# Dense layer's input rows: transposed as 16-bit parts by DMA in place of TensorE, from the third pair of tiles on

## The chip, the core and the metric

The kernel runs on one core of a Trainium2 chip: TensorE (PE) for products, VectorE (DVE), ScalarE (ACT) and GpSimd (POOL) for element-wise work, SyncE (SP) as the queue that issues nearly all DMAs. The metric is the device time of one execution in microseconds, the median over runs.

## The reference

Three layers follow one another. Shapes: q, k, v are 4 x 8 x 768 x 64 (batch, heads, positions, head size); 3072 tokens of 512 values each leave attention.

```python
scores = (q @ k.T) / 8 - slope[h] * dist      # keys: 8 global ones and the 96 before the query
a = exp(scores - max); a = a / sum(a)
x = (a @ v), as 3072 rows x 512
h = max(x @ w1, x @ w2, x @ w3)               # dense layer, 768 wide
x2 = h @ w_out                                # 3072 x 512
e = argmax(x2 @ w_gate)                       # one of 8 experts per token
out = gate * sigmoid(x2 @ w_output_gate)[e] * (relu(x2 @ e_w1[e]) @ e_w2[e])   # 1024 wide
```

## The kernel before

Tokens are handled in 24 tiles of 128 rows. All wide products are made of three 16-bit products: each operand is kept as a high part and a low part (`low_of` computes the low part as scaled value minus high part, with a running sum for a check at the end).

The first stage interleaves attention and the dense layer. Attention goes tile by tile (u = 0 to 23): loads of q, k, v (L823, L821), transposes of q and k on PE (L903), scores (L955), minima and exponentials (L979, L986), a split of the probabilities into two 16-bit parts (L1000), a DMA transpose of these (`a_trans`, L1006), products with v (L1036), and a scaled result `xo` (L1042) that is stored to a DRAM buffer `xd` (L1048).

The dense layer goes in 12 passes over pairs of tiles. `m_load(p, t)` fetches tile t of pair p: for the first two pairs (`NEARLY = 2`) the tile is still in SBUF, later ones are reloaded from `xd` (L1077). PE transposes its four 128x128 blocks in fp32 into a PSUM bank (L1089), ACT writes the scaled high part from there (L1092), DVE the low part (L1094, shown at L200). Both go to one of two `xT` buffers, and a pass needs both tiles of its pair. `m_1` makes the products with w1, w2, w3 (L1125); `m_max` takes maxima; `m_2` makes the product with w_out (L1182), writes its result as two 16-bit parts `x2r`, and transposes these through `rows_T` (L1218), a DMA transpose issued by SP (L1223; for the last pair PE does it). `m_route` then chooses experts and scatters the rows.

The order of all of this is made by a planner, the class `Plan`, when the program is built: tasks are generators that yield operations with an engine, an estimated cost and the buffers that they read and write; the planner picks the operation that can start first by its estimates (rank breaks ties), and the instructions are emitted in that order. On the chip each engine, SP's queue too, runs its own list in that fixed order and waits on semaphores. Buffers come from stocks: `take` waits for one, `give` returns it.

After the lists of tokens per expert are made, a loop over experts (L1881) runs to the end.

Of the kernel before, what the change touches and what calls it, by code (L numbers as in the profile page):

```python
# [9 lines left out]
F32 = mybir.dt.float32  # L10
F32R = mybir.dt.float32r
F16 = mybir.dt.float16
# [3 lines left out]
ALU = mybir.AluOpType  # L16
# [4 lines left out]
P = 128  # L21
# [11 lines left out]
NEARLY = 2  # L33
# [17 lines left out]
XS = 2.0**13  # L51
# [16 lines left out]
class Plan:  # L68
# [24 lines left out]
    def state(self, *fact):  # L93
        self.facts.add(fact)

    def give(self, tag, buf):
        buf.free = buf.last
        self.idle.setdefault(tag, []).append(buf)

    @staticmethod  # L100
    def need(*facts):
        return ("need", facts)

    @staticmethod
    def take(tag):
        return ("take", tag)

    @staticmethod
    def op(eng, cost, r=(), w=(), tail=None, port=True):
        return ("op", eng, cost, r, w, tail, port)  # L110
# [87 lines left out]
def low_of(nc, out, x, scale, high, total):  # L198

    nc.vector.scalar_tensor_tensor(out=out, in0=x, scalar=scale, in1=high, op0=ALU.mult, op1=ALU.subtract, accum_out=total)  # L200


def dense_attention(tc, q, k, v, vd, ngl, nlo, ident):

    nc = tc.nc
    B, H, S, HD = q.shape
    QT = S // P
    HS = S // 2
    with tc.tile_pool(name="da", bufs=1) as da, tc.tile_pool(name="db", bufs=1) as db, tc.tile_pool(
        name="dps", bufs=2, space=PSUM  # L210
# [4 lines left out]
        dist = da.tile([P, QT, S], F32, name="ddist")  # L215
        mask = da.tile([P, QT, S], F32, name="dmask")
# [1 line left out]
        nc.vector.tensor_scalar(out=mask, in0=dist, scalar1=0.0, scalar2=None, op0=ALU.is_ge)  # L218
        nc.vector.scalar_tensor_tensor(out=mask, in0=dist, scalar=nlo, in1=mask, op0=ALU.is_lt, op1=ALU.mult)
        nc.vector.tensor_mul(out=dist, in0=dist, in1=mask)  # L220
        for i in range(0, QT, 2):
            far = db.tile([P, 2, S], F32, tag="far", name="dfar")
            nc.vector.tensor_scalar(out=far, in0=mask[:, i : i + 2], scalar1=0.0, scalar2=nlo, op0=ALU.is_equal, op1=ALU.mult)
            nc.vector.tensor_add(out=dist[:, i : i + 2], in0=dist[:, i : i + 2], in1=far)
        nc.vector.tensor_max(out=mask, in0=mask, in1=glo.unsqueeze(1).to_broadcast([P, QT, S]))
        nc.vector.tensor_scalar(out=mask, in0=mask, scalar1=-MASK, scalar2=MASK, op0=ALU.mult, op1=ALU.add)
        slopes = da.tile([P, H], F32, name="slopes")
# [2 lines left out]
        with tc.For_i(0, B, 1) as b, tc.For_i(0, H, 1) as h:  # L230
# [9 lines left out]
            for src, dst, sc in ((qn, qT, -1.0 / HD**0.5), (kn, kT, 1.0)):  # L240
                for c in range(QT):
                    pt = dps.tile([P, 512], F32, tag="dpt", name="dpt")
                    nc.tensor.transpose(pt[:HD, :P], src[:, c, :], ident)
                    nc.scalar.mul(out=dst[:, c * P : (c + 1) * P], in_=pt[:HD, :P], mul=sc)
            for i in range(QT):
                t = db.tile([P, S], F32, tag="dt", name="dt")
                for half in range(2):
# [4 lines left out]
                        out=t[:, ks], in0=dist[:, i, ks], scalar=slope, in1=sc[:, :HS], op0=ALU.mult, op1=ALU.add  # L252
# [4 lines left out]
                    out=t, in0=t, in1=mask[:, i], scale=1.0, scalar=3.0e38, op0=ALU.add, op1=ALU.min, accum_out=mn[:, 0:1]  # L257
# [5 lines left out]
                for c in range(QT):  # L263
                    pt = dps.tile([P, 512], F32, tag="dpt", name="dpa")
# [3 lines left out]
                for c in range(QT):  # L268
# [4 lines left out]
                    out=vd[bass.ds(b, 1), bass.ds(h, 1), i * P : (i + 1) * P, :].rearrange("o u p d -> p (o u d)"), in_=o  # L273
# [105 lines left out]
def local_attention_moe_kernel(  # L379
# [17 lines left out]
    nc = tc.nc  # L397
    B, H, S, HD = q.shape
    NT, D = out.shape
    FF = w1.shape[1]  # L400
    E, _, FE = e_w1.shape
    KD = D // P
    KF = FF // P
    KE = FE // P
    QT = S // P
# [14 lines left out]
    ident = cp.tile([P, P], F32, name="ident")  # L420
# [17 lines left out]
    chk = cp.tile([P, -(-(A_OK + 8) // LINE) * LINE], F32, name="chk")  # L438
    late = ExitStack()
    big = late.enter_context(tc.tile_pool(name="big", bufs=1))  # L440
    mo = late.enter_context(tc.tile_pool(name="mo", bufs=1))
# [19 lines left out]
    with tc.manual_schedule(engines={mybir.EngineType.SP, mybir.EngineType.Activation}):  # L461
# [3 lines left out]
        for j, src in enumerate((q, k, v)):  # L465
            t = first_t[j // 2][:, j % 2 * D : (j % 2 + 1) * D]
# [31 lines left out]
    def window(nf, neg, gl):  # L498

        nc.vector.tensor_scalar(out=neg, in0=nf, scalar1=0.0, scalar2=4294967296.0, op0=ALU.is_lt, op1=ALU.mult)  # L500
        nc.vector.tensor_add(out=neg, in0=neg, in1=nf)
        nc.vector.scalar_tensor_tensor(out=gl, in0=nf[:, 1::2], scalar=4294967296.0, in1=neg[:, ::2], op0=ALU.mult, op1=ALU.add)
        return gl[:, 0:1], gl[:, 1:2]
# [7 lines left out]
    with tc.If(dense > 0):  # L511
        nf = cp.tile([P, 4], F32, name="nf")
        nc.vector.tensor_copy(out=nf, in_=nw)
        ngl, nlo = window(nf, neg, gl)
        dense_attention(tc, q, k, v, vd, ngl, nlo, ident)
# [5 lines left out]
    ngl, nlo = seen_gl[:, 0:1], seen_gl[:, 2:3]  # L521
# [3 lines left out]
    op, need, take, give, state = plan.op, plan.need, plan.take, plan.give, plan.state  # L525
    PE, DVE, ACT, POOL, DMA = "PE", "DVE", "ACT", "POOL", "DMA"

    def stock(tag, tiles, bank=False):
        for t in tiles:
            plan.idle.setdefault(tag, []).append(Buf(t, bank))  # L530
# [7 lines left out]
    def act(n):  # L538
        return 0.17 + n * 0.00085

    def dve(n):
        return 0.155 + n * 0.00104
# [4 lines left out]
    def psum(cost, r=(), w=()):  # L547

        return op(DVE, cost, r, w, port=False)

    def dma(nbytes, r=(), w=(), held=False, rate=DMA_RATE):
        return op(DMA, 0.5, r, w, tail=(0.06 + nbytes / rate, held))
# [29 lines left out]
    x2_all = mo.tile([P, 3 * XB], F32, name="x2r")  # L582
    x2_t = [x2_all[:, n * XB : n * XB + XW] for n in range(3)]
    stock("x", x_t)
    stock("x2s", [mo.tile([P, 2 * KD, 2 * P], F16, name="x2s")])
    stock("hm", hm_t)

# [476 lines left out]
    def m_load(p, t):  # L1064
        c = passes[p][0]
        n = CHUNKS[c][t]
        seq = X_SEQ[p] + t
        yield need(("o", n), *([("x", seq - 1)] if seq else []), *([("xT", p - 1)] if p else []))
        if p < NEARLY:
            xb = M["x", n]  # L1070
            state("x", seq)
        else:
            xb = yield take("x")
            state("x", seq)
            xb.free = max(xb.free, X_AT[n])
            yield dma(P * D * 4, w=[xb])
            nc.sync.dma_start(out=xb.t, in_=xd[n * P : (n + 1) * P, :])  # L1077
        if t == 0:
            M["xT", p] = yield take("xT")
            state("xT", p)  # L1080
        yield need(("xT", p))
        yield op(DVE, 0.2, [xb], [])
        nc.vector.tensor_reduce(out=chk[:, A_L + n : A_L + n + 1], in_=xb.t[:, :NLOW], axis=AX.X, op=ALU.max)
        xT = M["xT", p]
        bank = yield take("bank")
        pt = bank.t.rearrange("p (a b) -> p a b", b=P)
        for d in range(KD):
            yield op(PE, 0.109, [xb], [bank])
            nc.tensor.transpose(pt[:, d, :], xb.t[:, d * P : (d + 1) * P], ident)  # L1089
        h, l = [x[:, :, t * P : (t + 1) * P] for x in xT.t]  # L1090
        yield op(ACT, act(D), [bank], [xT])
        nc.scalar.mul(out=h, in_=pt, mul=XS)  # L1092
        yield psum(dve(D) + 0.07, [bank, xT], [xT])
        low_of(nc, l, pt, XS, h, chk[:, n : n + 1])  # L1094
        give("bank", bank)
        give("x", xb)
        state("xT", p, t)

    def m_banks():
# [118 lines left out]
    def rows_T(rows, src, dst, t, dstb, pe_, get=None):  # L1218

        at = dst[:, :, t * P : (t + 1) * P]  # L1220
        if not pe_:
            yield dma(P * 2 * D * 2, [src], [dstb], rate=DMA_RATE_ROWS)
            nc.sync.dma_start_transpose(out=at, in_=rows)  # L1223
            return
        bank = yield get()
        pt = bank.t.bitcast(F16).rearrange("p (a b) -> p a b", b=P)
        for d in range(2 * KD):
            yield op(PE, 0.06, [src], [bank])
            nc.tensor.transpose(pt[:, d, :], rows[:, d * P : (d + 1) * P], ident16)
        yield op(ACT, act(D), [bank], [dstb])  # L1230
        nc.scalar.copy(out=at[:, :KD], in_=pt[:, :KD])
        yield psum(dve(D), [bank], [dstb])
        nc.vector.tensor_copy(out=at[:, KD:], in_=pt[:, KD:])
        give("bank", bank)
# [586 lines left out]
    for p, (c, js) in enumerate(passes):  # L1821
        for t in range(len(CHUNKS[c])):
            plan.add(m_load(p, t), (1, p, -1, t), HOLD_M)
        plan.add(m_1(p), (4, p, 0), HOLD_F)
        if 2 in js:
            for t in range(len(CHUNKS[c])):
                plan.add(m_2(c, t), (4, c, 1 + t), HOLD_F)
# [12 lines left out]
    with tc.manual_schedule(engines={ET.PE, ET.Activation, ET.DVE, ET.Pool, ET.SP}):  # L1840

        reli, mask, tmp = [t[:, n * NW : (n + 1) * NW] for t, n in ((hm_t[0], 0), (hm_t[0], 1), (hm_t[1], 0))]
        key, rel, rel0, far, mask0, slopes = [hm_t[0][:, 2 * NW + n * NG : 2 * NW + (n + 1) * NG] for n in range(6)]
# [4 lines left out]
        for t, fill in ((rel, MASK), (rel0, 0.0)):  # L1848
            nc.gpsimd.affine_select(
                out=t, in_=rel0, pattern=[[-1, NG]], compare_op=ALU.is_ge, fill=fill, base=0, channel_multiplier=1  # L1850
# [3 lines left out]
        for j in range(2):  # L1854
# [4 lines left out]
            out=reli[:, NG:], in_=reli[:, NG:], pattern=band, compare_op=ALU.is_ge, fill=MASK, base=NPREV, channel_multiplier=1  # L1859
# [77 lines left out]
```

## Time and profile before

| what | value |
|---|---|
| median of 3 runs | 910.21 us (909.91 to 914.42) |
| profiled execution | 908.63 us, its span 907.1 us |
| PE busy | 829.1 us, 91% of the span |
| DVE busy | 641.0 us, 71% |
| ACT busy | 473.7 us, 52% |
| POOL busy | 197.8 us, 22% |
| DMA queue of SP | 65.1% of 16 engines' span |

The span runs from the first to the last instruction; the time of an execution contains a little more. Busy shares are means over stages: attention with dense products until about 450 us, dense products until about 570 us, experts from about 600 us on. PE's products are pipelined, so an instruction's duration is longer than the distance to the next one.

### The profile page before, as it was taken

The numbers are of one execution on the slowest core, as the hardware profiler recorded it, in microseconds if no ns is written. First come the engines' busy times: TensorE is split into PE (matmuls) and PEld (weight loads), VectorE is DVE, ScalarE is ACT, GpSimd is POOL, SyncE is SP. The second block draws the span as 40 slices with busy tenths as digits, with TensorE's granted clock in tenths as the row PEclk, the third lists the DMA queues.
The fourth block names the chain that finished last, engine by engine and source line by source line (L and its number), as shares of the span: only waits on it lengthen the run. The fifth ranks groups of instructions, "written<-read, shape, count | busy, mean of one in ns | idle before, by whom it ended". The sixth has DMA issues, their size and how long they took to land. (4 is left out here: it accounts for less than half of the span.)

```text
span 907.1 us, 23690 instructions
## 1 busy us (share of the span) xinstructions
PE 829.1 (91%) x8469; PEld 638.4 (70%) x8469; DVE 641.0 (71%) x1911; ACT 473.7 (52%) x994; POOL 197.8 (22%) x245
## 2 busy tenths in 40 slices
PE   3566799999999999999999999979999999989993
PEld 2456677787878786878778778747777766667671
DVE  5998968888788877877567523447677776657774
ACT  4776756667567666765344211205555555545551
POOL 3443332232324132211011011011111111111111
PEclk9968899999999999999999999989999999999997
DMA  7996459878797888874585131067888888888841
GB/s 206 267 252 198 106 89 205 177 189 182 159 197 188 172 209 170 185 165 99 130 322 143 24 60 36 13 233 214 245 256 255 255 247 243 260 247 246 246 133 38
DMA packets 271702, 164.58 MB, mean 181 GB/s; under 512 B 233824, under 2 KB 233824, under 8 KB 271620
## 3 DMA queue, kind: packets, MB, share of 16 engines
q1 hardware_dynamic: 267458, 150.91, 65.1%
q0 software_dynamic: 4160, 12.62, 3.8%
q8 instruction: 46, 0.75, 0.3%
q14 instruction: 36, 0.29, 0.1%
q10 hardware_dynamic: 2, 0.00, 0.0%
HBM read 118.56 MB, written 23.11 MB: 156 GB/s over the span
## 5 line engine op out<-in xcount | busy, mean ns | idle before, releaser
L1125 PE MATMUL bank<-xT,w 128*128 128x256 f16 x2592 | 306.4, 275 | 3.8 <-DVE xT L200 2.1
L1125 PEld LDWEIGHTS <-w 128*128 128x128 f16 x2592 | 250.4, 99 | 45.6 <-issue 9.8
L1689 PE MATMUL bank<-xT,we 128*128 128x128 f16 x2496 | 145.8, 222 | 13.2 <-DMA xT<-x2r 7.4
L1689 PEld LDWEIGHTS <-we 128*128 128x128 f16 x2496 | 143.8, 99 | 17.0 <-DMA xT<-x2r 8.3
L986 ACT ACTIVATE sp<-sp,mn 128x232 f32<-128x232 f32 (+1 forms) x192 | 89.8, 468 | 56.0 <-DVE mn L979 53.2
L1643 PEld LDWEIGHTS <-he 128*128 128x128 f16 x672 | 65.2, 98 | 75.7
L1632 ACT ACTIVATE hm<-bank 128x512 f32<-128x512 f32 x56 | 33.2, 593 | 137.3 <-PE bank L1689 121.3
L1182 PE MATMUL bank<-w,hh 128*128 128x512 f16 x432 | 101.0, 379 | 0.0
L1147 DVE SCALAR_TENSOR_TENSOR hm<-bank,hm 128x512 f32<-128x512 f32 x72 | 49.7, 690 | 57.8 <-PE bank L1125 55.0
L1643 PE MATMUL bank<-we,he 128*128 128x512 f16 x360 | 80.2, 379 | 0.0
L1182 PEld LDWEIGHTS <-hh 128*128 128x128 f16 x432 | 41.1, 98 | 40.7 <-issue 0.2
L1643 PE MATMUL bank<-wp,he 128*128 128x512 f16 x312 | 69.5, 379 | 0.0
L856 POOL TENSOR_SCALAR qkn<-qkn,vs 128x512 f32<-128x512 f32 x23 | 38.6, 1678 | 140.6 <-DVE vs L851 92.7
L200 DVE SCALAR_TENSOR_TENSOR wp<-ws,wp 128x1024 f16<-128x1024 f32 x56 | 65.2, 1220 | 0.0
L1319 POOL DMA_INDIRECT xs<-x2r,di x24 | 26.2, 1091 | 171.5 <-DVE x2r L1315 91.9
L979 DVE CUSTOM_DVE_ANT_0 sp<-bank,bias 128x232 f32<-128x232 f32 x160 | 60.5, 389 | 3.3 <-PE bank L955 3.2
L200 DVE SCALAR_TENSOR_TENSOR we<-ws,we 128x1024 f16<-128x1024 f32 x49 | 59.7, 1223 | 0.5
L955 PE MATMUL bank<-k,qh 64*128 64x232 f32 (+1 forms) x384 | 43.5, 317 | 18.0 <-ACT k L929 14.9
L195 POOL TENSOR_TENSOR seen<-x,dco 128x1 f32<-128x1 f32 x14 | 13.2, 940 | 208.6 <-DVE x L1648 208.6
L1574 ACT ACTIVATE wp<-ws 128x1024 f16<-128x1024 f32 x54 | 55.1, 1050 | 5.2 <-PE bank L1643 3.5
L1636 DVE CAST he<-hm 128x512 f16<-128x512 f32 x29 | 12.4, 427 | 62.7 <-ACT hm L1632 62.6
L195 DVE TENSOR_TENSOR nat<-sp,nat 128x928 f16<-128x928 f32 (+1 forms) x47 | 53.2, 1131 | 0.8
(260 smaller groups left out, 1232.7 us busy)
## 6 DMA issues: line engine op xcount, KB each, us to landing
ws<-in_moe_w_dram SPq DMA_DIRECT2D x112, 512.0 KB
raw<-in_moe_w_dram SPq DMA_DIRECT2D x12, 768.0 KB
bias<-in_moe_w_dram SPq DMA_DIRECT2D x16, 512.0 KB
x2r<-xs SPq DMA_DIRECT2D x30, 257.0 KB
qkn<-in_q_dram SPq DMA_DIRECT2D x23, 256.0 KB
qkn<-in_k_dram SPq DMA_DIRECT2D x23, 256.0 KB
qkn<-vd SPq DMA_DIRECT2D x23, 256.0 KB
qkn<-in_v_dram SPq DMA_DIRECT2D x23, 256.0 KB
```

What stands on the lines that cost most here:

```text
L195: eng.tensor_tensor(out=out, in0=in0, in1=in1, op=ALU.subtract)
L200: nc.vector.scalar_tensor_tensor(out=out, in0=x, scalar=scale, in1=high, op0=ALU.mult, op1=ALU.subtract, accum_out=total)
L856: nc.gpsimd.tensor_scalar(out=vf, in0=vf, scalar1=scale, scalar2=None, op0=ALU.mult)
L955: nc.tensor.matmul(sc[j][:, hp, :nw_], lhsT=x, rhs=y, start=(n < 2), stop=(n >= len(terms) - 2))
L979: nc.vector.tensor_tensor_reduce(out=o[:, g:], in0=x[:, g:], in1=bias[:, pr, n0 + g :], scale=scale, scalar=low, op0=ALU.add, op1=ALU.min, ...
L986: nc.scalar.activation(out=o, in_=o, func=AF.Exp, scale=-1.0, bias=mn[:, h : h + 1], accum_out=sm[:, h : h + 1])
L1125: nc.tensor.matmul(pj[:, f2, :], lhsT=w_at(j, part, d)[:, fs], rhs=X[:, d, :], start=(d + n == 0), stop=(d == KD - 1 and n == 2))
L1147: nc.vector.scalar_tensor_tensor(out=hv, in0=pj, scalar=1.0 / WS, in1=hv, op0=ALU.mult, op1=ALU.max)
L1182: nc.tensor.matmul(bank.t, lhsT=X[:, f, t * P : (t + 1) * P], rhs=w_at(3, part, f), start=(f + n == 0), stop=(f == KF - 1 and n == 2))
L1574: nc.scalar.mul(out=h, in_=s.t, mul=XS)
L1643: nc.tensor.matmul(py, lhsT=at(A_), rhs=w, start=(f + m == 0), stop=(last and m == 2))
L1689: nc.tensor.matmul(pg[:, f, :], lhsT=W[d][B_][:, fs], rhs=xT[A_][:, d, :], start=(d + m == 0), stop=(d == KD - 1 and m == 2))
```

## The change

For pairs from the third on, the tile is no longer transposed by PE. ACT writes the scaled high part of the untransposed tile to the left half of a new SBUF buffer `rows` (128 x 1024, 16 bit; one buffer), DVE the low part to the right half, the input buffer is given back, and `rows_T` issues one DMA transpose of all eight 128x128 blocks to the tile's place in `xT`. The buffer `rows` is given back to the planner after that transpose. Room for `rows` is made in a part that does not run with these inputs (`dense_attention`, used when the window is larger than the fast path's): its buffer `far` is halved.

```diff
-        for i in range(0, QT, 2):
-            far = db.tile([P, 2, S], F32, tag="far", name="dfar")
...
+        for i in range(QT):
+            far = db.tile([P, S], F32, tag="far", name="dfar")
...
     stock("x", x_t)
+    stock("rows", [mo.tile([P, 2 * D], F16, name="rows")])
...
         xT = M["xT", p]
-        bank = yield take("bank")
-        pt = bank.t.rearrange("p (a b) -> p a b", b=P)
-        for d in range(KD):
-            yield op(PE, 0.109, [xb], [bank])
-            nc.tensor.transpose(pt[:, d, :], xb.t[:, d * P : (d + 1) * P], ident)
...
+        if p < NEARLY:
...
+        else:
+            rows = yield take("rows")
+            yield op(ACT, act(D), [xb], [rows])
+            nc.scalar.mul(out=rows.t[:, :D], in_=xb.t, mul=XS)
+            yield op(DVE, dve(D) + 0.07, [xb, rows], [rows])
+            low_of(nc, rows.t[:, D:], xb.t, XS, rows.t[:, :D], chk[:, n : n + 1])
+            give("x", xb)
+            yield from rows_T(rows.t, rows, xT.full, t, xT, False)
+            give("rows", rows)
         state("xT", p, t)
```

The branch `p < NEARLY` holds the former lines unchanged.

## Rows read from the trace of the kernel before

**Rows 1.** The page: the span, and each engine's busy time.

```profile
span 907.1 us, 23690 instructions
PE 829.1 (91%) x8469; PEld 638.4 (70%) x8469; DVE 641.0 (71%) x1911; ACT 473.7 (52%) x994; POOL 197.8 (22%) x245
```

**Rows 2.** Busy time by stretches; last PE's granted clock, DMA share, GB/s.

```profile
150.00:450.00 300.00, 295.38 (x3145) 234.54 (x3146) 232.92 (x788) 186.85 (x496) 75.82 (x93) 1.00 0.78 173
450.00:607.00 157.00, 151.08 (x1213) 114.66 (x1211) 83.36 (x281) 40.84 (x70) 15.38 (x31) 0.99 0.36 108
```

**Rows 3.** Timeline of PE: start, length, operation, count, idle before and its releaser.

```profile
606.91 12.71 PE L1689 MATMUL bank<-xT,we 128*128 128x128 f16 x192 [5.77 <-SPq L1881]
```

**Rows 4.** Timeline of PE at the last pair's transposes.

```profile
500.76 0.60 PE L1089 MATMUL bank<-ident,x 128*128 128x128 f32 x4
501.20 0.60 PE L1089 MATMUL bank<-ident,wf 128*128 128x128 f32 x4
```

**Rows 5.** Instructions of line 1089, 169 to 605 us (ns: min/median/max).

```profile
L1089 PE MATMUL bank<-ident,x x44: 272/273/307, 188.2 to 501.1; 128*128 128x128 f32 x44
L1089 PE MATMUL bank<-ident,wf x28: 272/273/331, 169.2 to 501.5; 128*128 128x128 f32 x28
```

**Rows 6.** Timeline of PE at the start of the third pass.

```profile
163.87 1.15 PE L1125 MATMUL bank<-xT,w 128*128 128x256 f16 x9
...
169.15 0.66 PE L1089 MATMUL bank<-ident,wf 128*128 128x128 f32 x4 [1.21 <-DMA wf<-xd]
```

**Rows 7.** Groups by line: count, busy us, mean ns, idle before.

```profile
L1092 ACT ACTIVATE xT<-bank 128x512 f16<-128x512 f32 x24 | 14.0, 593 | 13.6 <-PE bank L1089 12.9 <-PE bank L842 0.7
L858 ACT CAST va<-qkn 128x512 f16<-128x512 f32 x23 | 14.1, 613 | 6.0 <-POOL qkn L856 5.9
L200 DVE SCALAR_TENSOR_TENSOR xT<-bank,xT 128x512 f16<-128x512 f32 x24 | 16.4, 687 | 3.7 <-ACT xT L1092 3.6
L200 DVE SCALAR_TENSOR_TENSOR he<-hm,he 128x512 f16<-128x512 f32 x56 | 38.8, 692 | 18.5 <-ACT he L1636 15.0
```

**Rows 8.** Instructions of line 1223, 150 to 450 us: issues on SP.

```profile
L1223 SPq DMA_TRANSPOSE x2s<-x2r x14: 1232/1434/2539, 166.7 to 443.4; - x14
```

**Rows 9.** Busy time in a quiet stretch with one such transpose.

```profile
541.50:545.50 4.00, 4.00 (x27) 2.48 (x26) 0.90 (x6) 0.60 (x2) 0.00 (x0) 1.00 0.35 66
```

**Rows 10.** Waits of SP's queue, 150 to 450 us: total, times, longest.

```profile
SPq L1006 <- DVE nat L195: 36.6, 15, 5.5
SPq L1006 <- DVE mn L979: 14.9, 5, 4.2
SPq L1048 <- DVE mn L979: 11.8, 6, 6.2
```

**Rows 11.** Waits of SP's queue over the whole span, the longest group.

```profile
SPq L1611 <- DMA xT<-x2r: 63.5, 26, 4.1
```

**Rows 12.** Timeline of PE: fourth pair's last transpose, first product of its pass.

```profile
188.68 0.31 PE L1089 MATMUL bank<-ident,x 128*128 128x128 f32 x1
...
213.45 2.78 PE L1125 MATMUL bank<-xT,w 128*128 128x256 f16 x24
```

**Rows 13.** Timeline of SP's queue: stores of attention's results and a transpose.

```profile
149.96 0.53 SPq L1048 DMA_DIRECT2D xd<-xo  x1
...
158.75 2.09 SPq L1006 DMA_TRANSPOSE aT<-nat  x1
160.88 0.85 SPq L1048 DMA_DIRECT2D xd<-xo  x1
...
445.77 0.35 SPq L1048 DMA_DIRECT2D xd<-wf  x1
```

**Rows 14.** Timeline of DVE: reading the third pair's second tile.

```profile
159.98 0.20 DVE L1083 TENSOR_REDUCE chk<-x 128x1 f32<-128x64 f32 x1
...
163.10 0.68 DVE L200 SCALAR_TENSOR_TENSOR xT<-bank,xT 128x512 f16<-128x512 f32 x1
```

More of the change, by code (lines that the diff above doesn't have):

```diff
@@ L220, in dense_attention @@
         nc.vector.tensor_mul(out=dist, in0=dist, in1=mask)
-        for i in range(0, QT, 2):
-            far = db.tile([P, 2, S], F32, tag="far", name="dfar")
-            nc.vector.tensor_scalar(out=far, in0=mask[:, i : i + 2], scalar1=0.0, scalar2=nlo, op0=ALU.is_equal, op1=ALU.mult)
-            nc.vector.tensor_add(out=dist[:, i : i + 2], in0=dist[:, i : i + 2], in1=far)
+        for i in range(QT):
+            far = db.tile([P, S], F32, tag="far", name="dfar")
+            nc.vector.tensor_scalar(out=far, in0=mask[:, i], scalar1=0.0, scalar2=nlo, op0=ALU.is_equal, op1=ALU.mult)
+            nc.vector.tensor_add(out=dist[:, i], in0=dist[:, i], in1=far)
         nc.vector.tensor_max(out=mask, in0=mask, in1=glo.unsqueeze(1).to_broadcast([P, QT, S]))
@@ L1084, in m_load @@
         xT = M["xT", p]
-        bank = yield take("bank")
-        pt = bank.t.rearrange("p (a b) -> p a b", b=P)
-        for d in range(KD):
-            yield op(PE, 0.109, [xb], [bank])
-            nc.tensor.transpose(pt[:, d, :], xb.t[:, d * P : (d + 1) * P], ident)
[L1090 to L1096, printed above, removed]
+        if p < NEARLY:
+            bank = yield take("bank")
+            pt = bank.t.rearrange("p (a b) -> p a b", b=P)
+            for d in range(KD):
+                yield op(PE, 0.109, [xb], [bank])
+                nc.tensor.transpose(pt[:, d, :], xb.t[:, d * P : (d + 1) * P], ident)
+            h, l = [x[:, :, t * P : (t + 1) * P] for x in xT.t]
+            yield op(ACT, act(D), [bank], [xT])
+            nc.scalar.mul(out=h, in_=pt, mul=XS)
+            yield psum(dve(D) + 0.07, [bank, xT], [xT])
+            low_of(nc, l, pt, XS, h, chk[:, n : n + 1])
+            give("bank", bank)
+            give("x", xb)
[5 more added lines that the diff above has]
+            low_of(nc, rows.t[:, D:], xb.t, XS, rows.t[:, :D], chk[:, n : n + 1])
+            give("x", xb)
+            yield from rows_T(rows.t, rows, xT.full, t, xT, False)
+            give("rows", rows)
         state("xT", p, t)
```

## The prediction

> **What bounds the kernel now.** I read the page first. TensorE (PE) is busy for 91% of the span [rows 1]. That is a mean over stages, so the table of stretches comes next: the change works between about 140 us (first input tile of the third pair) and 500 us (last one). From 150 to 450 us PE is busy 295.4 of 300 us; VectorE (DVE) 233, ScalarE (ACT) 187, the DMA queues 0.78, and PE's granted clock is 1.00, its 2.4 GHz level [rows 2]. In that stage PE is the limit, and what is taken off it comes off the end, provided that nothing new makes it wait: its order is fixed when the program is built, so a late operand stops it even if other products are ready. From 450 to 607 us nearly all is dense products, again with a full PE, and then comes the loop over experts, which the change does not touch. It can only start earlier: its first product at 606.9 us waited 5.8 us for SP's start of the loop, after the dense layer and the lists [rows 3].
>
> **What the change removes.** In the timeline of PE the four transposes of one tile begin at 500.76 us and those of the next at 501.20 us: 0.44 us a tile, 0.11 us each, although each lasts 272 ns by itself [rows 4, 5]. So the price on a full PE is the spacing, not the duration. After 165 us there are 44 + 28 = 72 such transposes, 18 tiles [rows 5]: 18 x 0.44 = 7.9 us off PE. The two tiles of the third pair are changed too (20 in all), but what they take off PE falls ahead of the wait described below and is worth nothing. One idle time goes as well: at 169.15 us PE stood 1.2 us until a reloaded input tile had landed, with dense products behind it [rows 6]. In the new kernel ACT and DVE wait for that tile, not PE. Together -9.1 us.
>
> The Trainium skill ("TensorE: Matmul & The Clock Gate", Part 4: PE-mode transpose) gives about 275 ns for one such transpose inside a kernel. The duration in the trace agrees (272 ns), but by it the sum would be 72 x 0.275 = 19.8 us (an estimate from that page); the spacing in the timeline is what I use.
>
> **What it adds on ACT and DVE.** Scaling and rounding moves from a PSUM bank to SBUF. ACT took 593 ns from PSUM for 128x512, and 613 ns for a cast of that size from SBUF; DVE's low part took 687 ns from PSUM and 692 ns in the line that reads SBUF [rows 7]. That is +0.02 and +0.005 us a tile, under 0.6 us over 20 tiles, on engines with 113 and 67 us to spare in the 300 [rows 2]: nothing. A PSUM bank less is held per tile; I count no gain. Both engines now stand in their order until the tile has landed, and ACT also until the one buffer for rows is free, which is when the previous transpose has landed. Behind them are exponentials and maxima of attention. The sum of such waits is what I cannot read; it stands in the rest term below.
>
> **What it adds on SP and the DMA queues.** One transpose of 128x1024 16-bit values per tile. The same operation exists: the results of the dense layer go that way. Issuing takes SP 1.23 us when all is quiet, 1.43 in the median between 150 and 450 us, at most 2.54 [rows 8]. In a quiet stretch of 4 us with one of them the queues were busy for 0.35: 1.4 us of all queues [rows 9]. Twenty of them are 28 us of queue time; 18 over the 300 us put the share from 0.78 to 0.86. SP has room too: its longest waits between 150 and 450 us, for DVE's low parts, minima and outputs, add up to 36.6 + 14.9 + 11.8 = 63 us [rows 10], against 18 x 1.43 = 26 us (46 by the maximum). From issue to landing: in the loop SP's next load waits for such a transpose, 63.5 us over 26 times, 2.4 each and at most 4.1 [rows 11], behind an issue of 1.23. So a tile becomes ready 3.7 to 5.3 us after SP takes up its transpose, instead of at the end of DVE's instruction.
>
> **Who waits for that.** A pass needs both tiles of a pair. There are two buffers for transposed input, so a pair is transposed while the pass before it runs. For the fourth pair the last transposes are at 188.7 us and its products start at 213.5 us: 25 us of cover [rows 12]. Later the cover grows, since attention (18 tiles from 149.96 to 445.77 us, 16.4 us each [rows 13]) runs ahead of the dense passes, and the last pair is transposed at 500.8 us with a whole pass running. Only the third pair has no cover: DVE's low part of its second tile starts at 163.10 us and lasts 0.68, and PE's first product of the pass starts at 163.87 us [rows 6, 14]. The tile was in SBUF by 159.98 us, when DVE reads it [rows 14]. In the new order ACT and DVE need 1.3 us from there, 161.3 us at best; SP is busy until 161.7 us with the transpose and the store that it issues from 158.75 us on [rows 13]; landing 3.7 us later is 165.4 us, with 5.3 us 167.0. Against 163.8 us the pass starts 1.6 to 3.2 us later, with little else for PE. I take the middle, +2.4 us.
>
> **The rest.** In-order waits of ACT, DVE and SP that reach PE. Below, nothing: PE's whole idle time in those 300 us is 4.6 us today, with the same kind of waits in it [rows 2]. Above, such a wait of 0.5 us a tile would cost 9 us. The evidence of spare time on every other engine puts it near the lower end: +1.5 us, with 0 to 9 kept for the range.
>
> Sum: -7.9 - 1.2 + 2.4 + 1.5 = -5.2 us. The profiled execution took 908.63 us (span 907.1 [rows 1] and 1.5 around it): 903.4 us. The three timed runs have a median of 910.21 us, 1.6 above the profiled one; since the sum is on the profile's scale and new runs will scatter upward in the same way, I give 904 us. One per cent is 9.1 us, so the whole gain from PE is hardly more than that. About 0.5% (4.6 us) is what a measurement of this kernel can tell from no change; against the median the bounds are 905.7 and 914.8 us.
>
> **Rivals.**
> A, the forecast: PE keeps its gain but for the third pair. 898 us (all of -9.1, a free start, and banks that help) to 905.7. Chance 0.50.
> B, no change: the gain is eaten by small waits. For it: PE's order is fixed, and each engine gets a new in-order wait per tile; 9.1 us are gone at 0.37 us a tile plus the late third pair. Against it: with such waits in today's order PE's idle time is 4.6 us in 300 [rows 2]. 908 us, within 905.7 to 914.8. Chance 0.28.
> C, slower by SP's queue: the new transpose stands in SP's order behind DVE's low part and the release of a buffer by PE; behind it are the loads of q, k and v and attention's own transposes, and PE's fixed order stops at attention's products. It decides from the point where the extra issue and wait of a tile exceed SP's spare time, 63/18 = 3.5 us [rows 10]; with 1.4 to 2.5 us of issue that leaves a wait of 1.0 to 2.1 us. One us beyond it per tile is 18 us on PE, less the 7.9 + 1.2: +9, 918 us. Waits of SP for PE's products exist already, but small. Chance 0.15.
> D, the transpose is far slower than its rows say, and the queues become the bound: today 0.22 x 300 = 66 us are free, 3.7 us a tile [rows 2], so it decides from a price of 3.7 us per tile. At 10 us, an example well beyond it, attention's tiles take 6.3 us longer, 113 us over 18; 55 us of that is covered (445.8 to 500.8 us), so about 58 - 9 = 49 us are lost: 958 us. The measured 1.4 us speaks against it. Chance 0.04. The Trainium skill ("VectorE: DVE Perf Modes", The three transpose paths) gives 1309 ns for one 128x128 block by DMA and advises TensorE where a PSUM destination will do; eight blocks at that price would be 10.5 us (an estimate from that page). Here eight blocks take 1.4 us of the queues [rows 9], so the trace disagrees with that price for a batch.
> E, the duration is the price of a PE transpose: 72 x 0.272 = 19.6 us, less the late pair: 891 us. The spacing speaks against it. Chance 0.03.
>
> **Numbers.** Faster by over 0.5%: A and E, 0.53. Within: B, 0.28. Slower: C and D, 0.19. The range 898 to 918 us holds A, B and the nearer half of C; D, E and the rest of C, about 0.15, are left out. The forecast's own range is 898 to 905.7 us.
>
> **What would show it.** The TensorE transposes of the input: 16 in place of 96, and 20 more DMA transposes. PE's busy time about 8 us less by 607 us, its first product of the third pass at 165 to 167 us, the expert loop's first product near 602 us. ACT and DVE unchanged in busy time, queue share 0.84 to 0.88 from 150 to 450 us. Wrong would be: idle time of PE ahead of attention's products with a releaser on the loads or attention's transposes (C), attention's tiles at more than 17.4 us each, or dense products that wait for a DMA at the start of a pass after the third.

## The result and the profile after

The changed kernel took 902.23 us in the median of four runs (901.14 to 903.04) against 911.89 us beside it: a ratio of 0.989 (95% interval 0.986 to 0.993). In two later comparisons of twelve runs each it was 0.993 (0.991 to 0.995) and 0.9925 (0.990 to 0.995), 6.4 and 6.6 us less. It is faster, by 0.7 to 1.1%. One execution with the dummy transposes, one in the other order and one of the kernel before fell into a slower state and are left out of all medians and ratios here. The forecast was 904 us, 0.7% under the median of before.

The busy time by stretches answers to [rows 2]; its third stretch is cut where the loop over experts begins.

```profile
150.00:450.00 300.00, 293.91 (x3120) 232.09 (x3118) 238.91 (x803) 184.21 (x499) 79.88 (x86) 1.00 0.87 186
450.00:601.50 151.50, 145.54 (x1166) 109.30 (x1162) 79.90 (x270) 42.23 (x69) 16.80 (x39) 0.99 0.42 123
601.50:901.50 300.00, 279.79 (x3121) 205.06 (x3121) 200.87 (x497) 146.91 (x182) 52.17 (x52) 0.97 0.75 225
```

TensorE (PE) is as full as before, the DMA queues went from 0.78 to 0.87, and the stretch before the loop is shorter. In PE's timeline, three places answer to [rows 3] and [rows 6]: the last input tile that PE still transposes (the same work in both kernels, at 104.80 us before), the first product of the third pass (163.87 us before) and the loop's first product (606.91 us before).

```profile
105.50 0.66 PE L1091 MATMUL bank<-ident,x 128*128 128x128 f32 x4 [1.05 <-DVE vs L845]
...
166.85 4.75 PE L1136 MATMUL bank<-xT,w 128*128 128x256 f16 x42 [0.30 <-DMA xT<-rows]
...
601.57 12.40 PE L1700 MATMUL bank<-xT,we 128*128 128x128 f16 x192 [5.94 <-SPq L1892]
```

From the first of these rows to the last I call it the stage; it leaves out the start, whose length scatters (this row stands at 104.3 to 106.4 us in the traces), and the loop. Line numbers are those of each kernel's own file. It took 606.91 - 104.80 = 502.1 us before and 601.57 - 105.50 = 496.1 us after: 6.0 us less. The loop took 300.2 us of span before and 299.9 after. So all of the difference between the two traces lies where the change acts. The two later traces of the changed kernel have stages of 497.0 and 497.9 us; the mean of three is 497.0, 5.1 us under before.

The new transposes, by the new line of `rows_T` (SP's time for an issue, least, median and most, in ns):

```profile
L1234 SPq DMA_TRANSPOSE xT<-rows x20: 1231/1319/4622, 151.0 to 501.2; - x20
```

and the split, by the tile `rows` (13 of the 20 tiles; the other seven come from the buffer `wf`, with medians of 620 and 681 ns):

```profile
L1102 ACT ACTIVATE rows<-x x13: 613/619/630, 146.2 to 493.7; 128x512 f16<-128x512 f32 x13
L200 DVE SCALAR_TENSOR_TENSOR rows<-x,rows x13: 672/685/1223, 147.2 to 495.2; 128x512 f16<-128x512 f32 x13
```

ACT needs 619 ns where it needed 593, DVE 685 where it needed 687 [rows 7]. SP issues in 1.32 us in the median, once in 4.6. What PE waited for between 130 and 600 us, in total, times and longest, is this after the change:

```profile
PE bank L1037 <- DMA aT<-nat: 3.1, 2, 2.1
PE bank L1037 <- ACT va L882: 1.3, 1, 1.3
PE bank L1295 <- DVE rt L1288: 0.8, 1, 0.8
PE bank L1037 <- POOL va L195: 0.3, 1, 0.3
PE bank L956 <- DVE ql L920: 0.3, 1, 0.3
PE bank L1136 <- DMA xT<-rows: 0.3, 1, 0.3
```

and was this before:

```profile
PE bank L842 <- ACT va L838: 3.3, 2, 1.9
PE bank L1089 <- DMA wf<-xd: 1.2, 1, 1.2
```

6.1 us against 4.5. All but the first line of after belong to the 17 us around the late start of the third pass. Attention's own DMA transposes (aT) are a new reason for PE to wait; the wait for a reloaded tile is gone. Attention's tiles take (451.96 - 152.31) / 18 = 16.6 us each (stores of its results, as in [rows 13]), against 16.4.

### The profile page after: what moved, and what is told of

It reads as the page before. It is cut to its first block, busy times and chain, and to the rows that moved or that the text cites. A ratio compares the mean times of both kernels' runs of the same rounds, so it can differ in the third digit from the quotient of the medians.

```text
span 901.5 us, 23553 instructions
## 1 busy us (share of the span) xinstructions
PE 822.8 (91%) x8389; PEld 631.3 (70%) x8389; DVE 642.6 (71%) x1912; ACT 471.2 (52%) x992; POOL 202.7 (22%) x246
## 5 line engine op out<-in xcount | busy, mean ns | idle before, releaser
L1700 PEld LDWEIGHTS <-we 128*128 128x128 f16 x2496 | 145.1, 100 | 16.4 <-DMA xT<-x2r 7.5
L200 DVE SCALAR_TENSOR_TENSOR we<-ws,we 128x1024 f16<-128x1024 f32 x49 | 59.8, 1223 | 0.5
L1647 DVE CAST he<-hm 128x512 f16<-128x512 f32 x29 | 12.4, 427 | 62.4 <-ACT hm L1643 62.3
L956 PEld LDWEIGHTS bank<-k,qh 64*128 64x128 f32 x384 | 32.4, 206 | 31.4 <-ACT k L930 16.0
```

The costliest lines, as they stand in the source:

```text
L956: nc.tensor.matmul(sc[j][:, hp, :nw_], lhsT=x, rhs=y, start=(n < 2), stop=(n >= len(terms) - 2))
L1700: nc.tensor.matmul(pg[:, f, :], lhsT=W[d][B_][:, fs], rhs=xT[A_][:, d, :], start=(d + m == 0), stop=(d == KD - 1 and m == 2))
```

## The experiments

My theory: the gain is PE's time, at the spacing of its transposes, less the late start of the third pass and some waits. Rivals: the gain comes from PSUM banks and eased ACT and DVE, or from a lucky order of the plan; and the cost side stands at the edge of SP's queue or of the DMA queues.

The stage and the loop of each kernel's trace (row of PE's fourth tile to the loop's first product, and from there to the end of the span), and the timed ratio to the kernel before (it is not the quotient of two medians and differs from it by up to 0.3%):

| kernel | stage us | to before | loop us | ratio (95%) |
|---|---|---|---|---|
| before | 502.1 | | 300.2 | 1 |
| changed kernel, three traces | 496.1, 497.0, 497.9 | -6.0, -5.1, -4.3 | 299.9, 303.6, 300.3 | 0.989, 0.993, 0.9925 |
| third pair on PE, two traces | 491.3, 494.6 | -10.8, -7.5 | 300.6, 299.5 | 0.9885 (0.985 to 0.992), 0.9865 (0.983 to 0.990) |
| last five pairs by DMA | 498.8 | -3.4 | 306.0 | 1.002 (0.999 to 1.005) |
| dummy PE transposes | 508.2 | +6.1 | 308.1 | 1.005 (1.003 to 1.0075) |
| results on PE | 506.2 | +4.1 | 302.6 | 1.005 (1.002 to 1.009) |
| other order | 495.1 | -7.1 | 305.3 | 0.996 (0.992 to 0.9996) |
| queue load | 503.6 | +1.5 | 297.5 | 0.997 (0.994 to 1.0004) |
| SP's wait | 507.6 | +5.5 | 299.9 | 1.008 (1.004 to 1.011) |
| each transpose twice | 523.9 | +21.8 | 303.9 | 1.018 (1.0125 to 1.024) |
| all pairs by DMA | no such row | | 306.1 | 0.991 (0.988 to 0.994) |

The edits below are cut to the line that matters. Six of the kernels (third pair on PE, last five pairs by DMA, dummies, results on PE, each transpose twice, all pairs by DMA) also carry this condition for the padding rows' stores, and the order of the work on SP, DVE and ACT differs in them from the changed kernel's from 163 us on or earlier; no run has the condition alone.

```diff
-            yield need(("o", QT + 1 + n))
+            yield need(("o", min(NTILE - 1, max(QT + 1 + n, 1 + max(u for u in range(NTILE) if ("o", u) in plan.facts)))))
```

**The changed kernel again**, beside the next three runs, and a third time beside the last three.

> The changed kernel once more, beside the next three. All theories: the ratio to the kernel before stays near 0.989, some 8 to 10 us less. Its sum on the profile's scale (5.2 us forecast, 6.0 us between the two traces) would be a ratio of 0.993 to 0.994; if the timed runs keep to 0.989, part of the gain lies outside of what the two traces show.

> The changed kernel beside the three others, as their base. Ratio to the kernel before between its two former values, 0.989 and 0.993; its stage up to the loop the same as in its two former traces within 1 us.

904.91 and 904.97 us in the median. The ratio went to 0.993, that of the sum, not to the first 0.989. The loop alone differs by 3.7 us between traces of one program, so part of the scatter of the timed runs (900 to 912 us) can be the loop's.

**The PE work put back.**

```diff
         else:
+            bank = yield take("bank")
+            pt = bank.t.rearrange("p (a b) -> p a b", b=P)
+            for d in range(KD):
+                yield op(PE, 0.109, [xb], [bank])
+                nc.tensor.transpose(pt[:, d, :], xb.t[:, d * P : (d + 1) * P], ident)
+            give("bank", bank)
             rows = yield take("rows")
```

> The changed kernel, and the four TensorE transposes of each tile are still made, into a PSUM bank that nobody reads. Theory: 20 x 0.44 = 8.8 us more than the changed kernel, so 0 to 3 us over the kernel before or equal to it (the costs of the change without its gain). Rival (the gain is the freed ScalarE and VectorE work on PSUM banks, or the order): stays within 3 us of the changed kernel.

915.73 us, 10.8 over the changed kernel in the same comparison; the stage 508.2 us, 11.2 over the mean of the changed kernel's. Where PE is full, what stands behind a tile's dummies starts 0.44 us after them:

```profile
212.31 0.60 PE L1104 MATMUL bank<-ident,x 128*128 128x128 f32 x4
212.75 0.93 PE L904 MATMUL bank<-ident,qkn 128*128 128x128 f32 x7
```

So 20 x 0.44 = 8.8 us is what the transposes should cost; PE's idle time from 130 to 600 us is 7.5 us in place of 5.9 in the mean, another 1.6. PE's granted clock adds some 2 us by estimate (0.83 from 160 to 180 us here; 1.00, 1.00 and 0.91 in the three traces of the changed kernel, the last with 0.91 from 240 to 260 us too). The three make 12.4 us, so the split of the 11.2 us holds within a microsecond or so. PE's longest waits:

```profile
PE bank L1142 <- DMA xT<-rows: 3.4, 1, 3.4
PE bank L1037 <- DMA aT<-nat: 1.7, 1, 1.7
PE bank L843 <- ACT va L839: 1.7, 2, 0.9
```

With PE's gain taken away, the change costs 4.5 us in the timed runs and 6.1 us in the stage. So the gain is PE's time, and not an ease on ACT, DVE and PSUM banks: a dummy's bank is held only until PE is done, without the reads of ACT and DVE, so most of that ease was still there.

**Another transpose moved, in the other direction.**

```diff
-        yield from rows_T(rows, x2, xs_.t, t, xs_, c == NCHUNK - 1, lambda: take("bank"))
+        yield from rows_T(rows, x2, xs_.t, t, xs_, True, lambda: take("bank"))
```

> The changed kernel, but the dense layer's results (22 tiles that went by DMA in both kernels) are transposed on TensorE, as the last pair's are. Theory (a transpose on a full TensorE costs its spacing): 8 blocks start 0.45 us apart per tile, 22 x 0.45 = 9.9 us more than the changed kernel in the stage (483 us), a ratio to the kernel before near 1.004. Rival (SP and the queues were short, so taking 22 transposes off them gives something back): less than 5 us more.

The stage is 9.2 us longer than the changed kernel's mean (0.42 us for each of 22 tiles, against 0.45 expected), the ratio 1.005. SP and the queues, 22 transposes lighter, gave nothing back.

**The third pair left on PE.**

```diff
-        if p < NEARLY:
+        if p < NEARLY + 1:
```

> The third pair stays on TensorE, DMA from the fourth pair on (18 tiles); the padding rows' stores are kept apart by a condition that alone leaves every engine's order as it is. Theory (the gain is TensorE time, the third pair's late start a loss of 2.3 us): the third pass starts near 164 us again and the time is 1.5 to 2.5 us under the changed kernel's, a ratio to the kernel before some 0.002 lower. Rival (the late start costs nothing since TensorE is filled otherwise): the same as the changed kernel or 0.9 us more.

> The version with the third pair on TensorE once more, beside the changed kernel. Theory (stage 5.7 us shorter than the changed kernel's in the traces, the loop the same but for its scatter): 4 to 7 us under the changed kernel, a ratio to the kernel before of 0.986 to 0.990. Rival (chance in the timed runs): within 2 us of it.

899.58 and 900.42 us, 5.3 and 4.6 under the changed kernel in the same comparisons: better than both kernels, and by more than the 1.5 to 2.5 us of the theory. In the first trace PE waited for nothing between 130 and 591 us; in the second four waits of 0.2 to 0.9 us are left, 2.3 us in all. The second stage is only 2.4 us shorter than the changed kernel's mean, the first 5.7.

By the first trace, two tiles cost 0.9 us on PE and 3.0 us of waits around the third pass go away, which is the 2.1 us expected. The rest is the 3.1 us of waits for attention's transposes at 250 and 420 us, which are gone in the first trace and 0.2 us in the second, and at neither place did this experiment change anything but the order. That the order is the reason is argued here, not shown.

**Only the last five pairs by DMA.**

```diff
-        if p < NEARLY:
+        if p < NEARLY + 5:
```

> Seven pairs on TensorE, the last five by DMA (10 tiles). Theory (0.44 us of TensorE per tile, no late third pair): 10 x 0.44 = 4.4 us under the kernel before, a ratio of 0.995. Rival (the gain comes from PSUM banks and a faster attention in the middle of the stage, not from TensorE time at the end): 0 to 2 us. Rival (a lucky order of the plan): no relation to the number of tiles.

The stage is 3.4 us shorter than before, near the 4.4 us of ten tiles. The timed runs say otherwise: 912.58 against 911.26 us, and the ratio of 0.995 that the theory gave lies outside the interval. The trace puts the difference into the loop, 306.0 us; its execution took 912.35 us, about the median of the timed runs, so a loop of that length is no exception here. For the timed runs the theory missed, and an influence of the order remains possible.

**The same work in another order.**

```diff
-    plan.add(pad_rows(), (5, 0), 0.5)
+    plan.add(pad_rows(), (5, 0), 0.8)
```

> The changed kernel with one number of the planner changed (the due time of the padding rows' stores, 0.5 to 0.8), which does the same work in another order on every engine from some point on. Theory (the gain is work taken off TensorE): within 3 us of the changed kernel in the stage, by idle times of TensorE alone. Rival (the gain is a lucky order): 5 us or more above it.

The stage is 1.9 us under the mean of the changed kernel's, so the order did not make the gain there. The order differs only from 230 us on for SP and from 298 us on for DVE and ACT, so this tests the later part of the stage. Timed, it kept less of it (0.996), again with a longer loop in its trace (305.3 us). No run took the kernel before in another order, so how far the order moves that side is not known.

**The cost side.** First each transpose issued twice, to the same place:

```diff
             yield from rows_T(rows.t, rows, xT.full, t, xT, False)
+            yield from rows_T(rows.t, rows, xT.full, t, xT, False)
```

> The changed kernel, with each tile's DMA transpose issued a second time to the same place (so SP waits for the first to land before it issues the second); the padding rows' stores have an earlier due time, since the plan could not be written otherwise. Per tile SP gets some 3.7 us more (1.23 of issue, 2.4 of wait) and the queues 1.4 us. Theory (SP and the queues have room, the dense passes are covered by the double buffer): from the changed kernel's time to 5 us more, the stage from 128 us to the loop's first product (473.5 us there) under 479 us. Rival (the changed kernel stands at the edge of SP's queue): 18 us more and beyond, with TensorE idle ahead of attention's products.

931.83 us, 17 over the kernel before: the rival was right and my estimate of SP's room wrong. The first lines of SP's waits and of PE's, 130 us on:

```profile
SPq L1235 <- DMA xT<-rows: 44.5, 17, 5.2
SPq L1007 <- PE bank L1137: 23.4, 9, 3.8
SPq L1007 <- PE bank L904: 15.4, 6, 3.3
...
PE bank L1137 <- DMA xT<-rows: 5.3, 1, 5.3
PE bank L904 <- DMA qkn<-in_q_dram: 4.0, 2, 2.1
```

SP waits 44.5 us for landings; PE waits for loads of q that come late, which it did nowhere in the changed kernel. The two possible causes were then tried one at a time, with every engine's order left as in the changed kernel. Both also bring issues of their own on SP, 20 of 0.63 us with the load and 20 of 0.25 us with the wait, so neither is quite alone:

```diff
             yield from rows_T(rows.t, rows, xT.full, t, xT, False)
+            nc.sync.dma_start(out=spare[n].rearrange("h t d -> t h d"), in_=q[0, :, 0:P, :].rearrange("h t d -> t h d"))
```

> The changed kernel in its own order on every engine, and behind each DMA transpose of an input tile SP issues one more transfer, 256 KB in pieces of 256 bytes from the input q to a buffer in DRAM that nobody reads: more load on the DMA queues (some 1.4 us of all queues per tile) and 0.4 us of issue, but no wait. Theory (in the run with each transpose issued twice SP's wait did the harm, 2.6 us in 17 cases): 0 to 5 us more than the changed kernel. Rival (the queues, then 0.87 busy in the stage, have no room for more): 10 us more and beyond, with TensorE idle ahead of attention's products behind loads and transposes.

```diff
             yield from rows_T(rows.t, rows, xT.full, t, xT, False)
+            nc.sync.dma_start(out=spare[n : n + 1, 0:32], in_=xT.full[0:1, 0, t * P : t * P + 32])
```

> The changed kernel in its own order, and behind each DMA transpose SP issues a transfer of 64 bytes out of the transposed tile, so that it waits for the landing, some 2.5 us per tile, with no load on the queues. Theory (SP's wait did the harm): 10 to 20 us more than the changed kernel, TensorE idle ahead of attention's products. Rival (the queues' load did): under 5 us more.

More load: 909.63 us, 4.7 over the changed kernel beside it, with the queues at 0.94, in the same stretch as above:

```profile
150.00:450.00 300.00, 292.83 (x3035) 229.53 (x3033) 235.95 (x791) 182.42 (x492) 78.37 (x86) 0.98 0.94 198
```

SP's timeline at the store of attention's last tile (at 451.96 us in the changed kernel, 445.77 before [rows 13]):

```profile
457.67 0.35 SPq L1050 DMA_DIRECT2D xd<-wf  x1
```

A wait with no load: 916.14 us, 11.2 over it, with the queues at 0.87 as in the changed kernel. The waits of SP and of PE:

```profile
SPq L1108 <- DMA xT<-rows: 37.4, 17, 4.1
...
PE bank L1038 <- DMA aT<-nat: 3.9, 4, 2.9
PE bank L1038 <- ACT va L883: 3.6, 5, 1.2
PE bank L1138 <- DMA xT<-rows: 1.5, 1, 1.5
```

and the same last store:

```profile
462.96 0.34 SPq L1050 DMA_DIRECT2D xd<-wf  x1
```

37.4 us of waiting on SP made attention end 11 us later and cost 11 us of time, 0.3 us for each us. Both causes count, SP's wait more; together 16 us, and each transpose twice cost some 24 (1.018 against 0.9925), there with another order as well.

Part of these costs stands beside a lower granted clock of PE (third number from the end). Two stretches, in the first trace of the changed kernel and then with more load:

```profile
160.00:180.00 20.00, 17.75 (x183) 13.84 (x183) 16.86 (x64) 12.55 (x36) 6.49 (x9) 1.00 0.91 201
240.00:260.00 20.00, 17.93 (x173) 12.54 (x172) 15.87 (x57) 10.12 (x29) 7.60 (x8) 1.00 0.91 175
...
160.00:180.00 20.00, 17.70 (x145) 12.59 (x144) 14.47 (x52) 11.33 (x31) 6.49 (x9) 0.83 0.91 203
240.00:260.00 20.00, 17.75 (x179) 14.01 (x179) 14.08 (x59) 9.43 (x26) 7.81 (x8) 0.91 1.00 194
```

With more load the clock is 0.50 from 168 to 173 us, its 1.2 GHz level, where PE had just waited 2.0 us for a tile of the third pair. With SP's wait the two stretches have 0.91 and 0.93. The missing share times 20 us, an estimate of the loss, is 5.2 us with the load and 3.2 us with the wait. PE's waits from 130 to 600 us are 8.0 and 12.6 us, against 6.1; the stages are 7.5 and 11.6 us longer than in the first trace. So in these traces the load's cost is mostly the lower clock, and the wait's cost mostly PE's waiting. The clock also falls without either: in the third trace of the changed kernel both stretches have 0.91, in the second 1.00. Why it falls in one execution and not in another stays open. With each transpose twice it is 0.97 from 130 to 600 us, some 14 us by the same estimate.

**All pairs by DMA.**

```diff
-        if p < NEARLY:
+        if p < 0:
```

> The first two pairs go by DMA too (24 tiles). Theory (without cover the latency shows): the first two passes start 3 to 5 us later each, against 4 x 0.44 us saved; the first product of the expert loop 2 to 7 us later than in the changed kernel. Rival (TensorE is not the limit before 130 us, so a later start there costs nothing): the same or 1 to 2 us less.

A ratio of 0.991, the loop's first product at 599.69 us against 601.57 to 603.38 in the three traces of the changed kernel. The rival was right: before 130 us PE waits for other engines anyway (in the kernel before it is busy 58.2 of the 70 us from 60 to 130 us), and a later start there cost nothing that shows.

## Why the prediction was right, and where it was not

**What bounds.** Right. Work put back on PE came back in full in the stage (11.2 us, where their spacing gives 8.8 and waits and clock account for the rest), and 22 other tiles gave 0.42 us each.

**The price of a transpose.** Right at 0.44 us a tile, the spacing; by the duration of 272 ns the dummies would have cost 20 x 4 x 0.272 = 22 us. The 275 ns of the Trainium skill ("TensorE: Matmul & The Clock Gate", Part 4: PE-mode transpose) agrees with the duration, though the page speaks of bf16 blocks and the blocks here have 32 bits, but it is no price on a full PE.

**ACT, DVE, the queues.** Right: +26 and -2 ns a tile, the queue share 0.87 for 0.86 forecast; PE waited for the new transposes only once, 0.3 us. The estimate of 10.5 us for eight blocks that I worked out from "VectorE: DVE Perf Modes" (The three transpose paths) of the Trainium skill does not hold here: SP takes 1.32 us per issue, and where it was made to wait for the landing, that came 37.4 / 17 = 2.2 us later.

**The third pair.** The start of its pass is later by (166.85 - 105.50) - (163.87 - 104.80) = 2.3 us in the first trace (3.3 and 3.4 in the later two); forecast 2.4. The term was sized by this start alone. Behind it PE waited another 1.3 us for ACT, since attention's products stand in the same fixed order; that makes 3.6. Leaving the pair on PE was worth some 5 us in the timed runs, 2.1 of them by the waits around this pass.

**The rest.** Forecast +1.5 us. In the first trace PE's waits grew by 1.6 us (6.1 against 4.5), but that contains the third pair's 3.0 and the 1.2 that went with the reloaded tile. What is left for this term is -0.2 us: the waits for ACT (3.3 us) went, waits for attention's transposes (3.1 us) came. That they cancel was luck; I had sized neither.

**The sum.** -5.2 us forecast; -6.0, -5.1 and -4.3 us in three traces of the stage. In the forecast's own terms the first trace has -7.9 - 1.2 + 3.6 - 0.2 = -5.7 us. So the sum is near by some luck: the third pair cost 1.2 us more than forecast and the rest 1.7 us less. The granted clock, for which the sum has no term, took some 3.6 us by estimate in the third trace. The timed runs gave 6.4 and 6.6 us, and 9.7 in the first comparison.

**The step that failed** is the one behind the rival C: "SP has room too: its longest waits", 63 us or 3.5 us a tile. These waits are room only in part. They stand at fixed places of the queue, and a new wait behind a transpose delays everything behind it. 2.2 us of wait a tile, close to the 1.0 to 2.1 us that I had called free, cost 11 us, some 3 of them beside the lower clock. The rest of the 37.4 us was taken up by waits that were there: SP's waits for DVE between 150 and 450 us, all rows added up, are 130 us in the changed kernel and 95 us with the added wait. The change is faster because its transposes bring an issue and no wait for a landing. SP does wait at them, 37.7 us in that stretch, but for DVE and other engines and not for a DMA; all its waits together are 162 us, against 185 before. One of the signs that I had named for C did show, in small: 3.1 us of PE ahead of attention's products behind attention's transposes. It was nearer to C than I said.

## What to carry to other kernels

On an engine that is full, a removed instruction is worth its spacing in the timeline; put the work back as a dummy to see whether that was the gain. Moving a transpose from TensorE to DMA pays where its landing is covered by a double buffer; where that engine is the limit, leave the pair whose consumer stands right behind it where it was. The waits in an in-order DMA queue are spare time only in part: load and one wait per tile must be tried one at a time, and here the wait cost more than twice the load. Read the granted clock of the stretch beside PE's waits, since part of such a cost can stand there.

## What the runs showed that I had not expected

The loop over experts, which no experiment changed, took 297.5 to 308.1 us in the traces, and 299.9, 303.6 and 300.3 us for one and the same program. In it PE waited for transposed rows, in the changed kernel:

```profile
PE bank L1700 <- DMA xT<-x2r: 6.7, 3, 3.8
```

and in the one with the last five pairs by DMA:

```profile
PE bank L1700 <- DMA xT<-x2r: 11.0, 6, 2.9
```

That is some 4 of the 6 us between these two. PE's idle time in the whole loop (its length less PE's busy time) is 20.1 us in the first and 25.2 us in the second, at granted clocks of 0.97 and 0.96; in the longest loop, with the dummies, it is 26.6 us at 0.96, in the shortest, with more load, 19.5 us at 0.97. So the difference is PE's waiting, with a small part of the clock. Why PE waits longer there after some orders of the first stage, and whether that repeats in timed runs (as 1.002 and 0.996 of two kernels with shorter stages suggest), stays open.
